# A static attention and convolution schedule: VectorE gets its own dispatcher, PV products lose their order, score groups become two or three, convolution halves are added on VectorE

## Chip, cores, metric

One NeuronCore of a Trainium2 (trn2) chip. The metric is the device time of one execution in microseconds; lower is better. "Fast" and "slow" are states of single runs: a run more than 1.5% above the fastest of the same kernel counts as slow and is left out of ratios. A *ratio* here is the mean time of one kernel's fast runs over the mean of the other's fast runs from the same rounds, so it is not quite the ratio of the medians quoted beside it.

Words used throughout: a *unit* is one block of scores, 128 keys by 512 queries of one head. There are 2048. A *chain* is the five-instruction exponential of one unit on VectorE, which takes it off ScalarE. The *PV product* multiplies a unit's probabilities with the values. A *filler* is a matmul on zeros whose result is not used.

## The reference, cut

```python
# A: short convolution, gate, long convolution (by FFT in the reference), gate
kv = k_shift * v                                   # k_shift: 4-tap causal filter of k; S=2048, D=640
y  = irfft2(rfft2(kv_pad) * rfft2(ssm_k_pad))[:S]  # a causal convolution of length 2048 per channel
a  = q * (y + kv * ssm_D)
# B: attention, 32 heads of 20
q, k, v = split(x @ wqkv)
p = softmax(q @ k.T * 20 ** -0.5)
b = (p @ v) @ wo
return concatenate([a, b], axis=-1)                # bf16 in and out
```

## The kernel before

The program is a list scheduler in Python. It keeps a clock for each engine (`P.T`), asks at each step which piece of work fits, and appends instructions with semaphore waits to each engine's list. What reaches the chip is the fixed order; nothing is decided there. The parts that matter:

```python
# score groups: pairs for the first 48 units, then fixed threes in banks 0-2 and 3-5
while n < NU:
    groups.append((n, min(3, NU - n), n % 6)); n += 3

def EXP_task(t, vec):                       # ScalarE takes 3 units, or 2 and VectorE one
    k, n, b0 = groups[t]; m = n - vec
    P.op("act", exp of m units ...)
    if vec:
        it = vexp_iter(k + m, b0 + m)
        next(it)                            # the chain's first step is put on VectorE's list at once
        chain.append([k + m, it])

def want_vec(t, now):                       # start a chain?
    if n < 3 or len(chain) > 1 or not 140 < k < NU - 30 or P.T["dve"] > now + 0.5:
        return 0
    ...

def PV_task(b):                             # strictly in order of b
    chain_end(4 * b + 3)                    # put the rest of any chain it needs on VectorE's list now
    ...

# end of each of 40 convolution tiles
P.op("dve", tensor_copy(zh, z1)); P.op("dve", tensor_tensor(zl, z1, zh, subtract))   # split into two bf16
for w, n, o, a in ((Win, 64, 0, zh), (Win, 64, 0, zl), (Wc, 60, 4, zh), (Wc, 60, 4, zl)):
    matmul(...)                             # shift by 32 partitions and add in PSUM
P.op("dve", tensor_copy(Y tile, sum))

# in the main loop, when nothing else fits: keep TensorE streaming
if sum(x[1] for x in P.stream) < 2.1 and slack > 0.45 and bnow > 1:
    zeros(...)
```

The kernel divides PSUM into eight banks: 0 to 5 for scores, one for the PV sums and one spare. Projections, transposes, output tiles and the convolution all use the spare one in turn. (cut: loads, first-stage convolution products, tail.)

The softmax here doesn't subtract the row's maximum and nothing guards it: scores larger than these inputs give would overflow.

Of the kernel before, what the change touches and what calls it, by code (L numbers as in the profile page):

```python
# [12 lines left out]
D = 640  # L13
H = 32
DH = 20
# [9 lines left out]
NHK = 5  # L25
# [4 lines left out]
KVPACE, CONV0, CONVE = 3, 500, 80  # L30
# [16 lines left out]
class Buf:  # L47
    def __init__(self, *alias):
        self.w = []
        self.r = []  # L50
        for a in alias:
            self.w += a.w + a.r


def RB(b):

    o = Buf()
    o.w = list(b.r)
    return o


class Prog:
    ENGS = ("sp", "act", "pe", "dve", "pool")

    def __init__(self, nc, enter):
        self.ops = {e: [] for e in self.ENGS}
        self.clock = {e: {} for e in self.ENGS}
        self.cnt = {}
        self.pend = {e: ([], []) for e in self.ENGS}
        self.enter = enter  # L70
        self.plast = None
        self.nc = nc
        self.T = {e: 0.0 for e in self.ENGS}
        self.dma_t = 0.0
        self.gap = None
        self.kind = None
        self.stream = []
        self.sem = {e: self.newsem("s_" + e) for e in self.ENGS if e != "sp"}
# [26 lines left out]
    def ready(self, eng, reads=(), writes=()):  # L105

        own = "s_pe" if eng == "pe" else None
        return max([t[4] for b in reads for t in b.w if t[0] != own] +
                   [t[4] for b in writes for t in b.w + b.r if t[0] != own] + [0.0])

    def op(self, eng, fn, reads=(), writes=(), tok=True, dsem=None, extra=(), n=1, c=0.1, kb=0.0, st=0.0, kind=None):
        own = self.sem[eng][0] if eng in self.sem else None
        if eng == "dve" and self.gap:

            f, self.gap = self.gap, None
            st = self.ready(eng, reads, writes)
            while self.T["dve"] + 0.5 < st and f(self.T["dve"]):
                pass
            self.gap = f
# [17 lines left out]
        if eng == "pe":  # L137
            if kind and kind == self.kind:
                c -= 0.1
            self.kind = kind  # L140
        waits = self._waits(eng, toks)
        start = max([self.T[eng]] + [t[4] for t in toks])
        self.T[eng] = start + c
        if st:
            self.stream.append((start, st))
        when = self.T[eng] + LAT.get(eng, 0.1)
# [63 lines left out]
def build_kernel(nc, A_q, A_k, A_v, A_shift_k, A_ssm_k, A_ssm_D, B_x, B_wqkv, B_wo, out):  # L210
# [3 lines left out]
    with ExitStack() as es:  # L214
# [20 lines left out]
        XI_sb = sb("XI", [128, 2, 512], I32)  # L235
        XZ_sb = sb("XZ", [128, 2, 512], FP32)
        Bout = sb("Bout", [128, 2, D])
# [3 lines left out]
        Win = sb("Win", [128, 128])  # L241
        Wc = sb("Wc", [128, 128])
        ZH = sb("ZH", [128, 2, 256])
        rden = sb("rden", [128, 2, 16], FP32)
# [38 lines left out]
        b_ident, b_Win, b_Wc, b_ones, b_tA, b_tB, b_C = (Buf() for _ in range(7))  # L283
# [5 lines left out]
        b_XI, b_XZ = [Buf(), Buf()], [Buf(), Buf()]  # L289
# [3 lines left out]
        b_On, b_rden = Buf(), [Buf(), Buf()]  # L293
# [29 lines left out]
        P.op("act", lambda e: e.activation(rden[:, 0, :], Zt[:, 0:16], ACT.Exp), reads=[b_Zt], writes=[b_rden[0]], c=1.6)  # L323
# [21 lines left out]
        def b_W(g, which="K"):  # L345
            return (b_WK0 if which == "K" else b_WQ0) if g == 0 else b_Wa if g == 1 else b_Wb


        def mbank():
            return min(mbanks(), key=lambda i: P.ready("pe", (), [bkb[i]]))  # L350

        def mbanks():
            return [MISC] + [OBANK] * (pv[0] == 0) + [4, 5] * (sofar() < NPAIR - 4)

        pv = [0]

        ev_i = [0]

        def XT_part(t, bk, c0, c1, eng, cost):
# [7 lines left out]
            P.op("pe", pe, reads=[b_x(t), b_ident], writes=[bkb[bk]], c=0.05 + 0.06 * (c1 - c0))  # L367
# [4 lines left out]
        def copy(eng, dst, src, bs, bd, cost):  # L372
            if eng == "act":
                P.op("act", lambda e: e.activation(dst, src, ACT.Copy), reads=[bs], writes=[bd], c=cost)
            else:
                P.op("dve", lambda e: e.tensor_copy(dst, src), reads=[bs], writes=[bd], c=cost)  # L376

        def XT_task(t):
            XT_part(t, mbank(), 0, NCC, "dve", 0.5)

        def KQ_mm(which, g, bk, x0, n):
            off = g * 4 * DH
            Wt = WQ if which == "Q" else WKV

            def pe(e):
                for cc in range(NCC):
                    for i in range(4):
                        ins = e.matmul(bank[bk][32 * i:32 * i + DH, 0:n],  # L388
                                       Wt[:, cc, off + i * DH:off + (i + 1) * DH], xT[:, cc, x0:x0 + n],
                                       start=(cc == 0), stop=(cc == NCC - 1), tile_position=(0, 32 * i))  # L390
                return ins
            P.op("pe", pe, reads=b_xT[x0 // 128:(x0 + n + 127) // 128] + [b_W(g, which)], writes=[bkb[bk]],
                 c=0.18 + 1.06 * n / 512, st=1.06 * n / 512)
# [33 lines left out]
        def KQ_task(which, g, c):  # L427
            bk = mbank()
            KQ_mm(which, g, bk, c * 512, 512)
            dst, bd = (QT[:, qs(c, g), :], b_QT[qs(c, g)]) if which == "Q" else (  # L430
                KT[:, g, c * 512:(c + 1) * 512], b_KT[(g, c)])
            copy("dve", dst, bank[bk], bkb[bk], bd, 0.7)
# [3 lines left out]
        def V_task(kb, z):  # L436
            bk = mbank()
            h0, nh = VZ[z]
            w = nh * DH

            def pe(e):
                for cc in range(NCC):
                    ins = e.matmul(bank[bk][:, 0:w], xT[:, cc, kb * 128:(kb + 1) * 128],  # L443
                                   WKV[:, cc, D + h0 * DH:D + h0 * DH + w],
                                   start=(cc == 0), stop=(cc == NCC - 1))
                return ins
            P.op("pe", pe, reads=[b_xT[kb], b_Wa if z == 0 else b_Wb], writes=[bkb[bk]], c=0.05 + 5 * w / 2400,
                 st=5 * w / 2400)
            P.op("dve", lambda e: e.tensor_copy(V_sb[:, kb, h0:h0 + nh, 0:DH],  # L449
                                                bank[bk][:, 0:w].rearrange("p (h d) -> p h d", d=DH)),  # L450
                 reads=[bkb[bk], b_ones], writes=[b_V[(kb, z)]], c=0.17 + w / 960)


        d_kst = [DS("kst0"), DS("kst1")]
        d_kvst = [DS("kvst0"), DS("kvst1")]
        d_kvr, d_sk, d_kext, d_small = DS("kvr"), DS("sk"), DS("kext"), DS("small")
# [11 lines left out]
        def kv_iter():  # L468

            def mul(o, a, b, op, reads, writes):  # L470
                P.op("dve", lambda e: e.tensor_tensor(o, a, b, op), reads=reads, writes=writes, c=0.49)  # L471

            for j in range(KS):
# [3 lines left out]
                     c=0.49)  # L477
# [21 lines left out]
        def setup_pool():  # L499
            P.op("pool", lambda e: e.memset(V_sb[:, :, :, DH:DH + 1], 1.0), writes=[b_ones])  # L500
            for t in (Win, Wc):
                bb = b_Win if t is Win else b_Wc
                P.op("pool", lambda e, t=t: e.memset(t, 0.0), writes=[bb])
                base = 32 if t is Win else -96
                P.op("pool", lambda e, t=t, base=base: e.affine_select(
                    out=t, in_=t, compare_op=ALU.not_equal, fill=1.0, base=base,
                    pattern=[[-1, 128]], channel_multiplier=1), reads=[bb], writes=[bb])
# [18 lines left out]
        groups, n = [], 0  # L526
        while n < NPAIR:
            groups.append((n, 2, n % 4))
            n += 2
        while n < NU:  # L530
            groups.append((n, min(3, NU - n), n % 6))
            n += 3

        def units(t):
            return range(groups[t][0], groups[t][0] + groups[t][1])

        def ubank(t, n):
            return groups[t][2] + n - groups[t][0]

        def S_needs(t):  # L540
            keys = []
            for n in units(t):
                qc, g, kb = qgk(n // 4)
                keys += [("Q", g, qc), ("K", g, kb // 4)]
            return keys

        def S_bufs(t):
            rd, wr = [], []
            for n in units(t):
                qc, g, kb = qgk(n // 4)  # L550
                rd += [x for x in (b_KT[(g, kb // 4)], b_QT[qs(qc, g)]) if x not in rd]
                wr.append(bkb[ubank(t, n)])
            return rd, wr

        def S_task(t):
            def pe(e):
                for n in units(t):
                    (qc, g, kb), u = qgk(n // 4), n % 4
                    ins = e.matmul(bank[ubank(t, n)], KT[32 * u:32 * u + DH, g, kb * 128:(kb + 1) * 128],  # L559
# [3 lines left out]
            rd, wr = S_bufs(t)  # L563
            P.op("pe", pe, reads=rd, writes=wr, c=0.32, st=0.22)

        def EXP_task(t, vec):
            k, n, b0 = groups[t]
            m = n - vec
            P.op("act", lambda e: e.activation(  # L569
                P_sb[:, k % NPU:k % NPU + m, :],  # L570
                PS[:, b0 * 512:(b0 + m) * 512].rearrange("p (u q) -> p u q", u=m), ACT.Exp, scale=scale),
                reads=[bkb[b0 + i] for i in range(m)], writes=[b_P[i % NPU] for i in units(t)[:m]], c=0.066 + 0.4217 * m)
            if vec:
                it = vexp_iter(k + m, b0 + m)
                next(it)
                chain.append([k + m, it])

        chain = []
        vn = [0]

        def vexp_iter(n, bk):


            i = vn[0] % 2
            vn[0] += 1
            XI, XZ, bi, bz = XI_sb[:, i, :], XZ_sb[:, i, :], b_XI[i], b_XZ[i]
# [6 lines left out]
            def step(fn, reads, writes):  # L593
                P.op("dve", fn, reads=reads, writes=writes, c=0.7)

            step(lambda e: e.tensor_scalar(XI, bank[bk], scale * 1.4426950408889634 * w, 127.0 * w, op0=ALU.mult, op1=ALU.add),  # L596
                 [bkb[bk]], [bi])
            yield
            step(lambda e: e.scalar_tensor_tensor(XZ, u, w * c2 / c3, u, op0=ALU.add, op1=ALU.mult), [bi], [bz])  # L599
            yield  # L600
            step(lambda e: e.scalar_tensor_tensor(XZ, XZ, w * w * c1 / c3, u, op0=ALU.add, op1=ALU.mult),  # L601
                 [bi, bz], [bz])
            yield
# [633 lines left out]
```

## Time and profile before

| | |
|---|---|
| time | median 945.38 us of 3 runs (936.87 to 946.68); later 942.39 of 4 |
| profiled run | span 937.6 us, mean granted TensorE clock 0.945 |
| ScalarE floor | 866.4 us (566 exponentials of three units, 125 of two; worked out in the prediction) |
| loss (span less floor) | 71.2 us |
| chains | 100 |
| fillers | 80, none between about 100 us and the end of the convolution |

How to read it: the floor is what ScalarE would take if it never waited. The rest of the span is loss. The prediction shows the lines this rests on; the granted clock by slices (tenths, 40 slices) is the one line that it didn't show:

```profile
PEclk9999999999998999979979999986799999999989
```

The clock records of this trace hold two values, 1.00 and 0.50. A slice is 23.4 us long and a 9 stands for 90% or more of full clock, so a 9 can hide up to 2 x 0.1 x 23.4 = 4.7 us at half clock. The 7s and the 6 are slices where more of the time ran at 0.50.

### The profile page before, as it was taken

What the parts mean: (1) busy time and instruction counts of PE and PEld (TensorE: products, weight loads), DVE (VectorE), ACT (ScalarE), POOL (GpSimd) and SP (SyncE); (2) the same over time, 40 slices, a digit from 0 to 9 for tenths busy, and PEclk for the clock granted to TensorE, in tenths of its full rate; (3) what the DMA queues carried; (4) which work ended last, traced back from release to release, by engine and by line L of the source; (5) the groups of instructions that cost most, each with busy time, mean ns of one, the idle gap of its engine ahead of it and who ended that gap; (6) DMA issues with size and microseconds to landing.
All of it is one profiled execution on the core that took longest, in us unless ns stands there. A gap on an engine that the chain in (4) does not pass through costs nothing.

```text
span 937.6 us, 25931 instructions
## 1 busy us (share of the span) xinstructions
PE 831.5 (89%) x11462; PEld 398.0 (42%) x11464; DVE 597.2 (64%) x1116; ACT 888.0 (95%) x699; POOL 123.9 (13%) x97
## 2 busy tenths in 40 slices
PE   9988888788988999899989999989998898899877
PEld 5333332224544555445535445444454454455222
DVE  4366766646665676866746767775677768667532
ACT  6999999999998999989999999997899999999995
POOL 3000000014220222102202102210202202200000
PEclk9999999999998999979979999986799999999989
DMA  9423343468633675645854656553465556364311
GB/s 288 153 86 122 126 133 119 153 86 206 180 101 108 156 180 155 169 114 140 164 116 126 162 149 167 157 158 94 128 159 150 134 151 154 101 157 122 85 49 52
DMA packets 82012, 129.14 MB, mean 138 GB/s; under 512 B 32977, under 2 KB 58699, under 8 KB 81899
## 3 DMA queue, kind: packets, MB, share of 16 engines
q1 hardware_dynamic: 79739, 124.36, 49.8%
q0 software_dynamic: 704, 2.74, 1.0%
q8 instruction: 90, 1.47, 0.7%
q10 hardware_dynamic: 1456, 0.37, 0.2%
q14 instruction: 23, 0.19, 0.1%
HBM read 116.81 MB, written 13.23 MB: 139 GB/s over the span
## 4 chain that ended last, share of the span: by engine, by line
ACT 62%; PE 30%; DVE 7%; issue 1%; DVEq 0%
ACT P_sb L569 62%; PE PS L859 10%; PE PS L559 8%; PE PS L627 6%; PE PS L388 2%; DVE P_sb L606 1%; PE PS L313 1%; PE PS L701 1%; DVE XZ L601 1%; DVE XI L604 1%; DVE XZ L599 1%; DVE ZH L872 1%; DVE ZH L873 1%; PE PS L880 1%; DVE R L902 0%
## 5 line engine op out<-in xcount | busy, mean ns | idle before, releaser
L569 ACT ACTIVATE P_sb<-PS 128x1536 bf16<-128x1536 f32 (+1 forms) x691 | 883.5, 1461 | 35.3 <-PE PS L559 34.0
L559 PE MATMUL PS<-QT,KT 20*128 20x512 bf16 x2048 | 278.4, 399 | 58.5 <-ACT P_sb L569 53.6
L859 PE MATMUL PS<-R 128*128 128x128 bf16 (+15 forms) x5120 | 244.7, 197 | 2.0 <-DVE O_norm L659 1.1
L859 PEld LDWEIGHTS PS<-R 128*128 128x128 bf16 x5120 | 202.0, 99 | 100.7 <-issue 100.7
L627 PE MATMUL PS<-P_sb,V_sb 128*21 128x512 bf16 x2048 | 174.2, 407 | 17.5 <-DVE P_sb L606 17.1
L827 POOL COPY R<-R 32x512 bf16<-32x512 bf16 x80 | 111.7, 1396 | 500.6 <-PE PS L859 488.7
L559 PEld LDWEIGHTS PS<-QT,KT 20*128 20x128 bf16 x2048 | 67.3, 91 | 212.2 <-ACT P_sb L569 157.8
L596 DVE TENSOR_SCALAR XI<-PS 128x512 int32<-128x512 f32 x100 | 69.1, 691 | 97.7 <-PE PS L559 97.6
L601 DVE SCALAR_TENSOR_TENSOR XZ<-XZ,XI 128x512 f32<-128x512 f32 x100 | 74.0, 740 | 2.4
L606 DVE SCALAR_TENSOR_TENSOR P_sb<-XZ,XI 128x512 uint16<-128x512 f32 x100 | 72.2, 722 | 1.7
L599 DVE SCALAR_TENSOR_TENSOR XZ<-XI 128x512 f32<-128x512 uint16 x100 | 72.2, 722 | 1.0
L627 PEld LDWEIGHTS PS<-P_sb,V_sb 128*21 128x21 bf16 x2048 | 33.2, 90 | 87.5 <-issue 54.7
L471 DVE TENSOR_TENSOR R<-R 128x640 bf16<-128x640 bf16 x128 | 61.4, 486 | 1.9
L604 DVE TENSOR_SCALAR XI<-XI 128x512 int16<-128x512 int16 x100 | 51.3, 513 | 2.0
L376 DVE CAST QT<-PS 128x512 bf16<-128x512 f32 (+1 forms) x32 | 21.8, 681 | 40.9 <-PE PS L388 40.9
L636 DVE CAST OT_sb<-PS 128x512 bf16<-128x512 f32 x32 | 22.1, 690 | 33.8 <-PE PS L627 33.8
L388 PE MATMUL PS<-xT,WQ 128*20 128x512 bf16 (+1 forms) x660 | 42.2, 387 | 0.5 <-DVE QT L376 0.4
L388 PE MATMUL PS<-xT,R 128*20 128x512 bf16 (+2 forms) x660 | 41.4, 381 | 0.5 <-DVE O_norm L659 0.3
L376 DVE CAST KT<-PS 128x512 bf16<-128x512 f32 (+1 forms) x32 | 21.7, 679 | 28.9 <-PE PS L388 28.9
L443 PE MATMUL PS<-R,xT 128*128 128x160 bf16 (+1 forms) x240 | 29.7, 257 | 4.2 <-DVE KT L376 1.4
L449 DVE CAST V_sb<-PS 128x160 bf16<-128x160 f32 (+1 forms) x48 | 18.4, 382 | 21.8 <-PE PS L443 21.4
L872 DVE CAST ZH<-PS 128x256 bf16<-128x256 f32 x40 | 17.0, 425 | 23.1 <-PE PS L859 22.7
(56 smaller groups left out, 351.7 us busy)
## 6 DMA issues: line engine op xcount, KB each, us to landing
R<-kext_scratch SPq DMA_DIRECT2D x640, 132.0 KB, 3.2
R<-in_A_k_dram SPq DMA_DIRECT2D x15, 640.0 KB, 3.9
kext_scratch<-in_A_ssm_k_dram POOLq DMA_DIRECT2D x1, 2560.0 KB, 13.0
R<-in_A_v_dram SPq DMA_DIRECT2D x16, 160.0 KB, 5.4
kv_scratch<-R SPq DMA_DIRECT2D x16, 160.0 KB
kvr_scratch<-R SPq DMA_DIRECT2D x16, 160.0 KB
R<-kvr_scratch SPq DMA_DIRECT2D x8, 320.0 KB, 6.6
R<-in_A_q_dram SPq DMA_DIRECT2D x32, 80.0 KB, 2.0
```

Of the source, the lines that this page charges most:

```text
L388: ins = e.matmul(bank[bk][32 * i:32 * i + DH, 0:n], Wt[:, cc, off + i * DH:off + (i + 1) * DH], xT[:, cc, x0:x0 + n], start=(cc == 0), sto ...
L471: P.op("dve", lambda e: e.tensor_tensor(o, a, b, op), reads=reads, writes=writes, c=0.49)
L559: ins = e.matmul(bank[ubank(t, n)], KT[32 * u:32 * u + DH, g, kb * 128:(kb + 1) * 128], QT[32 * u:32 * u + DH, qs(qc, g), :], start=True, ...
L569: P.op("act", lambda e: e.activation(P_sb[:, k % NPU:k % NPU + m, :], PS[:, b0 * 512:(b0 + m) * 512].rearrange("p (u q) -> p u q", u=m), A ...
L596: step(lambda e: e.tensor_scalar(XI, bank[bk], scale * 1.4426950408889634 * w, 127.0 * w, op0=ALU.mult, op1=ALU.add), [bkb[bk]], [bi])
L599: step(lambda e: e.scalar_tensor_tensor(XZ, u, w * c2 / c3, u, op0=ALU.add, op1=ALU.mult), [bi], [bz])
L601: step(lambda e: e.scalar_tensor_tensor(XZ, XZ, w * w * c1 / c3, u, op0=ALU.add, op1=ALU.mult), [bi, bz], [bz])
L604: step(lambda e: e.tensor_scalar(hi, hi, 128.0, None, op0=ALU.mult), [bi], [bi])
L606: step(lambda e: e.scalar_tensor_tensor(P_sb[:, n % NPU, :].bitcast(U16), XZ, 128.0 * c3 / w ** 3, hi, op0=ALU.mult, op1=ALU.add), [bi, bz ...
L627: ins = e.matmul(bank[OBANK][32 * u:32 * u + DH + 1, :], V_sb[:, kb, 4 * g + u, :], P_sb[:, (4 * b + u) % NPU, :], start=(kb == 0), stop=( ...
L827: P.op("pool", lambda e, dst=dst, src=src: e.tensor_copy(dst, src), reads=[cv["KVr"]], writes=[cv["KVX"][i]] if X == 3 else [], extra=(cv[ ...
L859: P.op("pe", lambda e, o=o, lhsT=lhsT, rhs=rhs, st=st, last=last: e.matmul(o, lhsT, rhs, start=st, stop=last, skip_group_check=True), read ...
```

## The change

Its intent: let VectorE take more units from ScalarE, and let nothing else stand in the way. (1) VectorE no longer gets instructions in the order in which they were thought of; a queue of pending work is served by readiness and priority. (2) PV products of a group run in any order of key blocks, and slots for probabilities come from a free list. (3) A score group is two or three units, and its third bank may be lent to projections. (4) The shift of the convolution's second half is done by two VectorE copies and an addition, not by shift matmuls. (5) Smaller: normalisations of two head groups are merged, output transposes and products repacked, and the filler rule is changed (threshold 1.8 us of streaming in 3.4 us, not 2.1 in 3.2; a convolution matmul counts with its columns alone, not 0.8 of its planned cost; which of the two brings in the fillers is not separated by any run). Projections and output products are also issued in small steps where the old program issued each as one block. Cut to the core:

```diff
-        groups, n = [], 0 ... fixed pairs and threes
+        S_task(ns, b0); EXP_task(k, m, vec, b0, got)      # m = 2 or 3, decided when issued
+    def spare(now):                                       # banks for side work
+            side = [2, 5] if nu[0] < NU - 24 and nu[0] >= NPAIR else []
+            return side + [MISC] * (not conv_wants(now))
-            it = vexp_iter(k + m, b0 + m); next(it); chain.append(...)
+            chain_start(k + m, b0 + m, got[m])            # five steps go to the queue
+    def dve_cands(now):                                   # dispatcher: ready time and priority of each
+        for w in works: ... yield max(T, r), pr, w
+    def want_vec(k, now):
+            if not 60 < k < NU - 34 or len(chains) >= NXB or not xfree: return 0
+            if ((k + 2) // 4) % NKB > 13 or micro_late(now - 1.5): return 0
+            return int(max(0.0, P.T["dve"] - now) + backlog() < VQ)     # VQ = 3.0, NXB = 3
-                    start=(kb == 0), stop=(kb == NKB - 1)
+                    start=first, stop=last                # PV: first and last issued, not by number
-                P.op("pe", four shift matmuls) ; copy
+            work(0.8, [copy M[0:64, 256:512] to ZS[64:128], shifted copy of M[64:128] to ZS[0:64],
+                       Y tile = M + ZS], after)
-                                st=0.8 * cost)
+                            st=2 * n / 2400)
-            if sum(x[1] for x in P.stream) < 2.1 and ...  # over 3.2 us
+            if sum(x[1] for x in P.stream) < ZTH and ...  # ZTH = 1.8, over 3.4 us
```

## The prediction

> **What bounds the kernel now.** I read the page's first two parts, then the chain of work that ended last, then the costliest groups, then the waits, then windows of ten microseconds and short timelines. Shares first:

> ```profile
> PE 831.5 (89%) x11462; PEld 398.0 (42%) x11464; DVE 597.2 (64%) x1116; ACT 888.0 (95%) x699; POOL 123.9 (13%) x97
> ...
> DVE  4366766646665676866746767775677768667532
> ACT  6999999999998999989999999997899999999995
> ...
> ACT 62%; PE 30%; DVE 7%; issue 1%; DVEq 0%
> ```

> ScalarE (ACT) is busy 95% of the span and carries 62% of the chain. VectorE (DVE) is busy 64%, and reaches 80% in only 2 of the 40 slices. ScalarE does nearly one thing, the exponential of 2048 score units of 128x512, except for 100 units that VectorE computes by a five-instruction chain:

> ```profile
> L569 ACT ACTIVATE P_sb<-PS 128x1536 bf16<-128x1536 f32 (+1 forms) x691 | 883.5, 1461 | 35.3 <-PE PS L559 34.0
> ...
> L596 DVE TENSOR_SCALAR XI<-PS 128x512 int32<-128x512 f32 x100 | 69.1, 691 | 97.7 <-PE PS L559 97.6
> L601 DVE SCALAR_TENSOR_TENSOR XZ<-XZ,XI 128x512 f32<-128x512 f32 x100 | 74.0, 740 | 2.4
> L606 DVE SCALAR_TENSOR_TENSOR P_sb<-XZ,XI 128x512 uint16<-128x512 f32 x100 | 72.2, 722 | 1.7
> L599 DVE SCALAR_TENSOR_TENSOR XZ<-XI 128x512 f32<-128x512 uint16 x100 | 72.2, 722 | 1.0
> ...
> L604 DVE TENSOR_SCALAR XI<-XI 128x512 int16<-128x512 int16 x100 | 51.3, 513 | 2.0
> ```

> The exponentials are 566 of three units and 125 of two. From their start times in the trace, the next one starts 1.331 us after one of three and 0.904 us after one of two when nothing is waited for, so a unit costs 0.427 us and an instruction 0.050 us more. The floor is 566 x 1.331 + 125 x 0.904 = 866 us. Summed over all exponentials, the excess over these intervals is 54 us; the other 17 us lie before the first and after the last. 866 + 54 + 17 = 937, the span. VectorE stands idle 97.7 us just before starting a chain: its static order puts the chain's first instruction ahead of other work that could run.

> Where the 54 us are lost is seen by comparing windows (after the time: busy of PE, PEld, DVE, ACT, POOL; granted clock; DMA share; GB/s):

> ```profile
> 400.00:410.00 10.00, 10.00 (x108) 4.98 (x106) 4.79 (x9) 7.05 (x6) 0.10 (x1) 0.50 0.29 71
> ...
> 430.00:440.00 10.00, 8.99 (x153) 4.98 (x150) 5.39 (x10) 10.00 (x10) 2.78 (x3) 1.00 0.16 49
> ```

> At full clock ScalarE is busy all ten microseconds; at half clock TensorE is busy throughout and ScalarE gets only 7.05. The 100 us from 600 lose most (89.21 us of ScalarE work at a mean clock of 0.83). A smaller loss is the PV product waiting for the chain's last step:

> ```profile
> PEld PS L627 <- DVE P_sb L606: 26.2, 33, 3.0
> ...
> PE PS L627 <- DVE P_sb L606: 17.1, 22, 2.7
> ```

> PV products are taken in strict order, [...] so one late chain holds up later scores as well.

> [...] 0.945 over the span means about 2 x 0.055 x 937.6 = 103 us at half rate. [...] of two independent steps the second starts 0.61 us after the first, which lasts 0.69:

> ```profile
> 332.63 0.69 DVE L596 TENSOR_SCALAR XI<-PS 128x512 int32<-128x512 f32 x1 [0.48 <-PE PS L559]
> 333.24 0.68 DVE L601 SCALAR_TENSOR_TENSOR XZ<-XZ,XI 128x512 f32<-128x512 f32 x1
> ```

> [...] the chain's last step has a median of 0.692 us and a maximum of 1.243. [...]

> **The change, part by part.**
> Convolution halves. Now each of 40 tiles makes two VectorE instructions (0.425 + 0.424), four shift matmuls and a third (0.424). After: copy, shifted copy and addition, three of about the same size, so VectorE stays at 40 x 1.27 = 51 us. TensorE loses the shift matmuls, 160 of them at 256 or 240 columns; busy 15.9 + 15.0 = 31 us in the profile, some 17 us of array time, and one round trip per tile through VectorE. TensorE isn't the bound at full clock, so this is slack for scores, worth perhaps 3 us.
> Merged normalisation, transposes and output projection. VectorE's instructions for these fall from 32+32, 16 and 24 to 17+17, 11 and 15; [...] (0.255 us for only 16 elements) it saves about 7 us of VectorE.
> Dispatcher. VectorE's 97.7 us of idle before chains become usable, a chain is begun when VectorE has under 3 us of work queued, three chains may be open in place of two, and chains are allowed from unit 60, not 140. How many chains this gives is the size on which all rests; the schedule decides it, so I estimate it. Chains are possible from about 35 us to 20 us before the end, some 850 us. VectorE's other work is 597.2 - 338.8 (the five rows above) = 258 us, less about 19 outside that stretch and 7 saved: 232. I take VectorE as 91% filled (no chain begins for the last two of every 16 key blocks, when the other VectorE work is late, or when the third bank is lent out): 774 - 232 = 542 us. A chain costs 3.39 us of busy time now; interleaved, it can save up to 5 x 0.08 us and one slow collision, so 2.95. 542 / 2.95 = 184 chains, 84 more than now.
> Groups of two or three. Lending the third bank to projections and taking pairs costs ScalarE more instructions. With 184 threes with a chain, 24 opening pairs, and the remaining 2000 - 552 = 1448 units at a mean of 2.75 (527), there are 735 exponentials, 44 more.
> PV in any order. It takes the 43 us of TensorE and weight-load waiting for chains mostly away. Little of it sets the end: I count it as offset by tighter coupling.
> Sum for ScalarE: (2048 - 184) x 0.427 + 735 x 0.050 = 796 + 37 = 833 us, against 866 before: 33 less. Losses stay at 54 + 17 = 71: time at half clock is not addressed, while less conv work but more scores per microsecond press on TensorE. 833 + 71 = 904. The profile lies at the low end of the three times (936.87 to 946.68, median 945.38), which I lay to the clock; the new kernel should spread likewise, so I add 2: **906 us**, 4% faster.

> **The rivals.**
> (1) VectorE becomes the bound. At 91% it has no reserve for the GpSimd copies (111.7 us in all, and they delay its steps); then scores wait for the bank that a chain hasn't read and PV for chains. For it: the waits above exist already at 64%. Against it: PV may go round a late chain, and chains are only begun on a short queue. It would add 20 to 30 us of losses: 925 to 935.
> (2) TensorE becomes the bound. It is busy 89%, and scores come 4% denser with more small groups and switches. Against it: at full clock windows keep ScalarE at 10.00 of 10, convolution work fills gaps wherever it fits, and the shift matmuls go. If half-clock time grows by half, losses grow by some 15 us: 920.
> (3) The chains don't come. If the lent bank, 24 slots for probabilities or the quota for other work hold them at 130, ScalarE's gain is 30 x 0.427 less the added instructions, about 11 us: 930, within 2%.
> (4) Better: 205 chains (VectorE 96% filled, 2.85 us each) and losses of 55: 787 + 37 + 55 = 879.

> **Range and chances.** (4) gives the low end near 882. (2) and a mild form of (1) give the high end, 926. 2% faster is 926.5, so faster takes nearly all above the lower tail: 0.86 faster, 0.11 within 2%, 0.03 slower.

> **What would show each step.** Chain steps x160 to x210 each; VectorE busy over 85%, its idle before the chain's first step under 40 us; ScalarE busy near 850 us with 700 to 780 exponentials; its waits for scores still 30 to 50 us, mostly at half clock; no shift matmuls; PV waits on chains under 20 us. I am wrong if chains stay under 140, if ScalarE's loss grows past 90 us, or if the chain of work that ended last has VectorE above 25%.

Four statements of the prediction with what the trace of the kernel before shows for them:

- A late chain holds up later scores: in the longest wait of a PV product for a chain, TensorE stood idle for 2.69 us, until 817.03 us, and the next scores started after the PV product, at 817.36.
- Chain steps that ran beside a GpSimd copy took longer (the prediction's delays and slow collision): the last step took a median of 0.857 us in the 17 cases in which it overlapped a copy (L827), and 0.691 in the other 83, at most 0.694. The other three steps that read SBUF alone had medians of 1.18, 1.47 and 0.92 us in the 10, 9 and 12 cases with a copy beside them, against 0.68, 0.69 and 0.46. The first step, which reads PSUM, took 0.692 us with or without one.
- The shift matmuls' array time: back to back at full clock they start 109 to 120 ns apart with 256 columns and 103 with 240 (L880), so 80 x 0.114 + 80 x 0.103 = 17 us.
- The 7 us saved by merging were an estimate; the 0.255 us for 16 elements is the reciprocal (L656).

## The result and the profile after

894.99 us, median of 4 runs (891.19 to 898.71), against 942.39 (936.87 to 946.68, 4 runs): ratio of fast runs 0.949, 95% interval 0.943 to 0.955. On another chip the same kernel ran 888.84 us (6 runs) against 938.78, ratio 0.948. The predicted 906 was 11 us too high, within the range.

The page's first parts, then the chain that ended last:

```profile
PE 835.4 (94%) x11432; PEld 388.0 (44%) x11432; DVE 785.4 (88%) x1427; ACT 856.0 (96%) x737; POOL 126.5 (14%) x94
...
DVE  4569999999699999998999999899999999999752
ACT  6699999999799999998999999999999999999996
...
PEclk9999999999699999999999999999999999999999
...
ACT 48%; DVE 30%; PE 20%; issue 1%; DVEq 0%
```

ScalarE is busy 32 us less (856.0 against 888.0), VectorE 188 us more, and the clock row has one slice that is not a 9. VectorE carries 30% of the last chain against 7% before: it has become a second bound. The costliest groups (busy, mean ns of one, then idle before them):

```profile
L639 ACT ACTIVATE P_sb<-PS 128x1536 bf16<-128x1536 f32 (+1 forms) x729 | 851.5, 1417 | 19.1 <-PE PS L597 18.4
...
L666 DVE TENSOR_SCALAR XI<-PS 128x512 int32<-128x512 f32 x171 | 117.0, 684 | 17.4 <-PE PS L597 16.8
L671 DVE SCALAR_TENSOR_TENSOR XZ<-XZ,XI 128x512 f32<-128x512 f32 x171 | 128.1, 749 | 0.0
L673 DVE SCALAR_TENSOR_TENSOR P_sb<-XZ,XI 128x512 uint16<-128x512 f32 x171 | 120.9, 707 | 4.9
L668 DVE SCALAR_TENSOR_TENSOR XZ<-XI 128x512 f32<-128x512 uint16 x171 | 123.0, 719 | 0.4
L670 DVE TENSOR_SCALAR XI<-XI 128x512 int16<-128x512 int16 x171 | 93.2, 545 | 0.0
...
L348 PE MATMUL PS<-Zt 128*128 128x512 bf16 x208 | 63.6, 402 | 1.5 <-DVE Zt L342 1.0
```

There are 171 chains and 729 exponentials. VectorE's idle time before a chain's first step is 17.4 us, against 97.7. The last line is the one to notice: 208 fillers, where the kernel before had 80. The waits of PV products for a chain's last step (us in total, times, longest):

```profile
PEld PS L692 <- DVE P_sb L673: 16.6, 39, 1.0
...
PE PS L692 <- DVE P_sb L673: 4.8, 14, 0.7
```

21.4 us, against 43.3. A piece of VectorE's timeline (start us, us) shows the dispatcher at work:

```profile
299.87 0.68 DVE L666 TENSOR_SCALAR XI<-PS 128x512 int32<-128x512 f32 x1
300.47 0.45 DVE L670 TENSOR_SCALAR XI<-XI 128x512 int16<-128x512 int16 x1
300.81 0.68 DVE L671 SCALAR_TENSOR_TENSOR XZ<-XZ,XI 128x512 f32<-128x512 f32 x1
301.41 0.68 DVE L702 CAST OT_sb<-PS 128x512 bf16<-128x512 f32 x1
302.01 0.68 DVE L673 SCALAR_TENSOR_TENSOR P_sb<-XZ,XI 128x512 uint16<-128x512 f32 x1
```

Steps of different chains and an evacuation follow each other: after one of 0.68 us the next starts 0.60 us later, after the one of 0.45 us 0.34 us later, so independent neighbours overlap. Over the whole trace the overlap of VectorE instructions is 78 us, against 29 before, so 237 us more of instruction time cost only 188 us more of busy time.

Two terms add up to the change of the profiled span, 48.3 us. By form the exponentials are 419 of three and 310 of two, so the floor is 419 x 1.331 + 310 x 0.904 = 837.9 us, which is 28.5 less. The loss is 889.3 - 837.9 = 51.4 us, which is 19.8 less. The time at half clock, from the clock records of the two traces, fell from 102 to 24 us within the span (the recorded expectations below count whole records, which reach 2 us past its end, and say 104). I had foreseen the first term and not the second, so the experiments ask what each is due to.

### The profile page after: what moved, and what is told of

Its sections match the earlier page's. It is cut to its first block, busy times and chain, and to the rows that moved or that the text cites. A ratio compares the mean times of both kernels' runs of the same rounds, so it can differ in the third digit from the quotient of the medians.

```text
span 889.3 us, 26279 instructions
## 1 busy us (share of the span) xinstructions
PE 835.4 (94%) x11432; PEld 388.0 (44%) x11432; DVE 785.4 (88%) x1427; ACT 856.0 (96%) x737; POOL 126.5 (14%) x94
## 3 DMA queue, kind: packets, MB, share of 16 engines
q8 instruction: 90, 1.47, 0.7%
## 4 chain that ended last, share of the span: by engine, by line
ACT 48%; DVE 30%; PE 20%; issue 1%; DVEq 0%
ACT P_sb L639 48%; PE PS L931 7%; PE PS L597 6%; DVE P_sb L673 5%; DVE XI L666 5%; DVE XZ L668 5%; DVE XZ L671 5%; DVE XI L670 4%; PE PS L692 3%; PE PS L445 2%; DVE R L952 1%; PE PS L348 1%; DVE ZS L950 1%; DVE ZS L949 1%; DVE OT_sb L702 1%
## 5 line engine op out<-in xcount | busy, mean ns | idle before, releaser
L639 ACT ACTIVATE P_sb<-PS 128x1536 bf16<-128x1536 f32 (+1 forms) x729 | 851.5, 1417 | 19.1 <-PE PS L597 18.4
L597 PE MATMUL PS<-QT,KT 20*128 20x512 bf16 x2048 | 286.5, 388 | 30.6 <-ACT P_sb L639 21.7
L666 DVE TENSOR_SCALAR XI<-PS 128x512 int32<-128x512 f32 x171 | 117.0, 684 | 17.4 <-PE PS L597 16.8
L671 DVE SCALAR_TENSOR_TENSOR XZ<-XZ,XI 128x512 f32<-128x512 f32 x171 | 128.1, 749 | 0.0
L673 DVE SCALAR_TENSOR_TENSOR P_sb<-XZ,XI 128x512 uint16<-128x512 f32 x171 | 120.9, 707 | 4.9
L668 DVE SCALAR_TENSOR_TENSOR XZ<-XI 128x512 f32<-128x512 uint16 x171 | 123.0, 719 | 0.4
L670 DVE TENSOR_SCALAR XI<-XI 128x512 int16<-128x512 int16 x171 | 93.2, 545 | 0.0
L692 PEld LDWEIGHTS PS<-P_sb,V_sb 128*21 128x21 bf16 x2048 | 37.6, 89 | 79.4 <-issue 50.4
L348 PE MATMUL PS<-Zt 128*128 128x512 bf16 x208 | 63.6, 402 | 1.5 <-DVE Zt L342 1.0
L530 DVE TENSOR_TENSOR R<-R 128x640 bf16<-128x640 bf16 x128 | 61.6, 487 | 3.7 <-DMA R<-in_A_v_dram 0.9
L445 PE MATMUL PS<-xT,WQ 128*20 128x512 bf16 (+1 forms) x660 | 48.9, 385 | 3.6 <-DVE R L952 1.7
L431 DVE CAST KT<-PS 128x512 bf16<-128x512 f32 (+1 forms) x32 | 21.4, 673 | 11.1 <-PE PS L445 11.1
```

The source lines that it names most:

```text
L348: P.op("pe", lambda e: e.matmul(bank[bk], Zt, zrhs, start=start, stop=start, skip_group_check=True), reads=[b_Zt], writes=[bkb[bk]], tok=s ...
L445: ins = e.matmul(bank[bk][32 * i:32 * i + DH, 0:n], Wt[:, cc, off + i * DH:off + (i + 1) * DH], xT[:, cc, x0:x0 + n], start=(cc == 0), sto ...
L597: ins = e.matmul(bank[b0 + i], KT[32 * u:32 * u + DH, g, kb * 128:(kb + 1) * 128], QT[32 * u:32 * u + DH, qs(qc, g), :], start=True, stop= ...
L639: P.op("act", lambda e: e.activation(P_sb[:, s0:s0 + m, :], PS[:, b0 * 512:(b0 + m) * 512].rearrange("p (u q) -> p u q", u=m), ACT.Exp, sc ...
L666: (lambda e: e.tensor_scalar(XI, bank[bk], scale * 1.4426950408889634 * w, 127.0 * w, op0=ALU.mult, op1=ALU.add), [bkb[bk]], [bl, bh], 0.6 ...
L668: (lambda e: e.scalar_tensor_tensor(XZ, u, w * c2 / c3, u, op0=ALU.add, op1=ALU.mult), [bl], [bz], 0.69, True),
```

## The experiments

Twelve runs were made: the changed kernel again, and eleven edits. "Clock" is the mean granted clock of the fast runs; medians are over all runs. 1, 2, 3, 7, 11 and 12 were run five rounds, the others three. 1 to 4 ran on one chip, 5 to 8 on a second and 9 to 12 on a third, each with the kernel before beside them, so across these groups compare ratios. The scheduler plans anew for each edit: an edit also moves other work, so no run changes one part with all else exactly in place.

| kernel | median us | ratio to before | clock, fast runs | chains | fillers |
|---|---|---|---|---|---|
| before (938.78 to 940.53 in these calls) | | 1 | 0.928 to 0.958 | 100 | 80 |
| after, repeated | 888.84 | 0.948 | 0.977 to 0.994 | 171 | 208 |
| after, no fillers while convolving | 953.88 | 1.014 | 0.887 to 0.896 | 172 | 80 |
| after, more fillers | 891.06 | 0.950 | 0.981 to 0.998 | 171 | 312 |
| after, chains held to 97 | 914.95 | 0.974 | 0.994 to 0.996 | 97 | 322 |
| after, PV in order | 906.28 | 0.963 | 0.977 to 0.989 | 176 | 250 |
| after, no lending (wrong result) | 962.03 | 1.022 | 0.989 to 0.994 | 184 | 384 |
| before, new convolution end | 984.30 | 1.045 | 0.881 to 0.895 | 102 | 112 |
| before, looser chain rule | 971.42 | 1.026 | 0.918 to 0.920 | 103 | 50 |
| before, new convolution end and zeros in its place | 975.63 | 1.037 | 0.912 to 0.922 | 99 | 118 + 80 |
| before, zeros behind the shift matmuls | 952.01 | 1.014 | 0.936 to 0.947 | 104 | 50 + 80 |
| after, PV first at the start | 906.49 | 0.961 | 0.971 to 0.986 | 174 | 214 |
| after, PV first and other settings | 874.43 | 0.933 | 0.994 to 1.000 | 181 | 248 |

**1. The changed kernel again**, no edit, as the yardstick for the next three.

> The changed kernel unaltered, as the yardstick for the three others on the same chip. Expected 890 to 899 us, 171 chains, clock 0.975 to 0.99. If its clock here falls to 0.95 as in the kernel before, the clock difference between the two first profiles was chance and the time should rise to about 905 us.

888.84 us, 1 us below the forecast, at a clock of 0.977 to 0.994. The better clock is not chance: no fast run of the kernel before was above 0.958.

**2. No fillers while convolution tiles remain.**

```diff
-            if sum(x[1] for x in P.stream) < ZTH and slack > 0.45 and bnow > 1:
+            if sum(x[1] for x in P.stream) < ZTH and slack > 0.45 and bnow > 1 and conv_b == 40:
```

> The changed kernel with the filler matmuls on zeros forbidden while convolution tiles remain: 80 zero matmuls instead of 208, as many as the kernel before has, none of them between 100 and 800 us. Chains stay at 172. Theory F (fillers keep the clock up): the granted clock falls to about 0.95, ScalarE loses 10 to 20 us more, time 905 to 915. Theory D (denser real work with fewer switches keeps it up): clock stays at 0.975 or more, time within 4 us of the changed kernel. Theory C (chance): no relation between the fillers and the clock in the repeated runs.

953.88 us: 65 us slower than the changed kernel, and 1.4% slower than the kernel before (interval 0.7 to 2.2%). The profile of a fast run:

```profile
PE 869.5 (91%) x11304; PEld 406.6 (43%) x11304; DVE 792.4 (83%) x1432; ACT 865.5 (91%) x735; POOL 126.0 (13%) x94
...
PEclk9998898899799999999999898897689958657999
...
L639 ACT ACTIVATE P_sb<-PS 128x1536 bf16<-128x1536 f32 (+1 forms) x727 | 861.0, 1339 | 70.3 <-PE PS L597 68.9
```

The floor is unchanged (422 x 1.331 + 305 x 0.904 = 837.4 us), but ScalarE stands idle 70.3 us before its exponentials instead of 19.1 (68.9 and 18.4 of it for scores), and the clock row is dented from end to end: 212 us at half clock. Theory F holds, and by four times the size I had given it. The other theory, that denser work alone keeps the clock up, falls: this kernel has the denser work and the worst clock but one. From the first profile of the changed kernel to this one the loss grows by 113.0 - 51.4 = 61.6 us and half-clock time by 188 us, so each microsecond at half clock costs about a third of one. The traces allow a check: book each exponential's delay beyond 1.331 or 0.904 us to the clock of that moment. At half clock the delays sum to 64.1 us here and 7.4 in the changed kernel, at full clock to 34.0 and 28.3. So all but 6 us of the added delay lies at half clock, and little is left for the new order by itself.

**3. More fillers.**

```diff
-... ZTH ... = 1.8
+... ZTH ... = 2.2          (and the guard described in 5)
```

> The changed kernel with the filler threshold raised from 1.8 to 2.2 us of streaming in the last 3.4 us: 312 zero matmuls instead of 208, 171 chains as before. (It also has a guard that a projection still under way does not count as done; alone, that guard leaves the schedule's counts unchanged.) Theory F: half-clock time goes to nearly nothing (clock 0.99 or more), time 2 to 6 us shorter. Theory D: clock and time unchanged within 3 us, or slightly slower since the fillers take TensorE time.

891.06 us, 2 us from the changed kernel and inside both spreads. The clock rises to 0.981 to 0.998 and nothing is gained: the other part of theory F's forecast, 2 to 6 us, isn't there. 208 fillers already leave little to win.

**4. Chains held to 97.**

```diff
+            if nvec[0] >= 100 * (k - 60) / (NU - 94):
+                return 0
             return int(max(0.0, P.T["dve"] - now) + backlog() < VQ)
```

> The changed kernel with the number of VectorE chains held to 97, spread evenly, everything else kept; the plan then has 531 exponentials of three and 179 of two, so ScalarE's floor is 531 x 1.331 + 179 x 0.904 = 868.6 us against 837.9. If the chains are what shortens ScalarE's work: time rises by about 31 us, to 920 to 930. If the gain came from better packing and not from the chains: less than 10 us slower. If the clock stays high here with few chains, the clock gain is independent of them, and the kernel should still be some 15 us faster than the kernel before.

914.95 us, 26 us above the changed kernel on the same chip, for a floor that is 30.7 us higher. This measures the chains, with one thing beside them: this kernel has 322 fillers, which by 3 moves the time little. It also gives the rest: with 97 chains, about as many as the kernel before, this one is 24 us faster than it. Booked as in 2, its delays at half clock are 2.8 us against 32.6 in the kernel before, and at full clock 25.0 against 22.9, so this rest lies in the clock. Its clock row and last chain:

```profile
PEclk9999999999999999999999999999999999999999
...
ACT 85%; PE 8%; DVE 3%; DMA 1%; POOL 1%; SPq 0%; issue 0%; DVEq 0%
```

With fillers in place and VectorE not pressed, ScalarE carries 85% of the chain, and the loss is 912.1 - 868.6 = 43.5 us, 5 us under that of 1 (48.3), which is why 30.7 us of floor cost only 26. This is what a schedule bound by ScalarE alone looks like.

**5. PV products in order again.**

```diff
-                if V not yet projected: continue
+                if V not yet projected: break
-                if P.ready("pe", rd, ...) <= now + 0.02:
-                    ok.append(b)
+                if P.ready("pe", rd, ...) > now + 0.02:
+                    break
+                ok.append(b)
```

> The changed kernel with PV products forced into the order of the key blocks again, the rest kept: 176 chains, 428 exponentials of three and 294 of two, floor 835 us. If free order matters: TensorE waits for the chain's last step rise from 21 us towards the 43 us of the kernel before, and the time by 5 to 12 us. If it does not: within 3 us of the changed kernel.

906.28 us, ratio 0.963 against 0.948: about 14 us slower, a little more than I allowed. Waits of PV products for the chain's last step rise to 33.6 us (21.4 in the changed kernel). The clock explains little: its run at 0.987 took 903.8 us, and the changed kernel's at 0.988, on the other chip, took 889.0.

A first build of the next experiment read keys before they were written, and was stopped. The scheduler counts a projection as done when its first matmul is placed, so a score may be placed ahead of the projection's end. The shipped order happens not to do that. The guard (a projection under way is not done) leaves the changed kernel's counts of exponentials, chains and fillers unchanged; it is in 3, 6, 11 and 12. 11 and 12 have one guard more: the last PV product of a head group waits for pending normalisations.

**6. No lending of the third bank.**

```diff
-            side = [2, 5] if nu[0] < NU - 24 and nu[0] >= NPAIR else []
+            side = []
```

> The changed kernel without lending: projections, transposes and output tiles get only the one spare bank, while that is not wanted by the convolution. 184 chains, floor 831 us, lower than in the changed kernel. (It has the guard for unfinished projections, without which this order read keys before they were written.) If lending is only a convenience: within 10 us of the changed kernel, since the floor is 7 us lower. If the bank is what lets side work run beside the convolution: the convolution is pushed back, VectorE and TensorE work is left over at the end, 40 to 70 us slower.

The result was wrong (relative error 1.0), so its time counts only as the time of this stream of instructions. A likely cause is that normalisations come so late here that the tile they read is overwritten; I didn't show it, and a guarded version found no schedule (that attempt is not on record). The time, 962.03 us, is 73 us above the changed kernel's on the other chip (ratios 1.022 and 0.948) though the floor is 7 us lower and the clock is 0.99:

```profile
L639 ACT ACTIVATE P_sb<-PS 128x1536 bf16<-128x1536 f32 (+1 forms) x695 | 844.1, 1465 | 99.3 <-PE PS L597 98.8
```

ScalarE's waits for scores are 98.8 us. In the longest, 9.6 us up to 693.45 us, TensorE finishes a convolution tile in the spare bank, then computes a query projection in that bank, and only then the scores that need it. As far as a kernel with a wrong result can tell, nothing of the gain would be left without the lending.

**7. The new convolution end alone, in the kernel before** (with the layout of the first-stage products that it needs).

```diff
-                copy, subtract, four shift matmuls, copy
+                copy M[0:64,256:512] -> ZS[64:128]; shifted copy M[64:128] -> ZS[0:64]; Y = M + ZS
```

> The kernel before with only the convolution's end changed: two copies into a float tile and an addition on VectorE in place of two copies, four shift matmuls and a copy. 102 chains, floor 865.5 us against 866.4. My step: TensorE was not the bound, so 0 to 5 us faster, 934 to 942. Rival: the shift matmuls and their round trip held the spare bank long enough to cost more, 8 to 15 us faster.

984.30 us, 4.5% slower than the kernel before, where I had said 0 to 5 us faster. The floor is about the same (865.5), the fast runs' clock is 0.881 to 0.895. The clock row of the profiled run, which was a slow one (995.3 us; its time is not used):

```profile
PEclk9999999997879886867689999698786977877988
```

**8. A looser rule for chains, in the kernel before.**

```diff
-  len(chain) > 1 or not 140 < k < NU - 30 or P.T["dve"] > now + 0.5
+  len(chain) > 1 or not 60 < k < NU - 30 or P.T["dve"] > now + 1.5
```

> The kernel before with only its rule for starting chains loosened: from unit 60 instead of 140 and with VectorE up to 1.5 us behind instead of 0.5. If VectorE's idle time alone was the resource, this should give more chains and a faster kernel. The old fixed groups with the old order give only 103 chains, and I expect the chains to sit in front of evacuations that TensorE needs: 15 to 30 us slower than the kernel before, which would show that the dispatcher, not the rule, makes the chains possible.

971.42 us over its four runs, 964 in the two fast ones, with 103 chains. As expected: at this setting the old fixed order places hardly more chains though it is allowed to. Its clock fell too (0.92), so the slowdown is not only the chains' place.

**9 and 10. Was it the shift matmuls that kept the clock up?** In 9, two zero matmuls of 512 columns stand where the four shift matmuls stood; in 10 they are added to the kernel before. Back to back at full clock, matmuls on zeros of 512 columns start 216 ns apart in the trace before (L313), so 80 of them are some 17 us.

```diff
+  for _ in range(2):
+      matmul(bank[MISC], Zt, zrhs, start=False, ...)      # adds zero
```

> The kernel with only the convolution's end moved to VectorE (984 us, 266 us at half clock), and at the place of the four shift matmuls of each tile two matmuls on zeros of 512 columns, that add zero to the convolution's bank: 80 in all, some 17 us of array time and no result. Theory A (the shift matmuls were dense work that kept the clock up, and their loss is what made that kernel slow): half-clock time falls from 266 us to about 100 to 150, time 940 to 955. Theory B (the new convolution end is itself slower in the old order, through its VectorE waits): half-clock time and time stay, 975 or more.

> The kernel before, with two matmuls on zeros of 512 columns added behind the four shift matmuls of each of the 40 tiles. Theory A: half-clock time falls from 104 us to 30 to 60. ScalarE's loss beyond its floor of 865 us should follow the relation seen so far, about 45 us plus 0.32 us for each us at half clock, so 55 to 65 us: 922 to 935 us. Against it: the old order has TensorE full at full clock, and the 17 us more array time push the convolution later (the plan grows by 13 us), so the time may stay at 940 although the clock is better.

The first took 968 to 977 us in its three fast runs, clock 0.912 to 0.922, so about 163 us at half clock (2 x 0.084 x 973) against about 221 (2 x 0.1126 x 982) in the fast runs of 7. That is the direction of theory A at half its size at most, and only 9 us. The second was slower than the kernel before, 952.01, at a clock no better. So dense work put in at one fixed place is not the cure, and theory A explains a part at most. Why the order with the new end has so many thin windows stays open.

One run of 9, the profiled one, had a span of 1626.5 us and is listed with a clock of 1.000. But its trace holds no clock record at all, and the 1.000 only says that none was found. Its matmuls tell more (line, shapes, count, then busy us, mean ns of one):

```profile
L551 PE MATMUL PS<-QT,KT 20*128 20x512 bf16 x2048 | 454.6, 668 | 2.2 <-ACT P_sb L561 2.0
L619 PE MATMUL PS<-P_sb,V_sb 128*21 128x512 bf16 x2048 | 318.2, 697 | 13.9 <-DVE P_sb L598 13.7
```

668 and 697 ns where the kernel before has 399 and 407, and consecutive full-array matmuls of 512 columns never start less than 0.36 us apart, where 0.216 is usual at full clock (L313 in the trace before; 0.427 at half clock). This run is in no comparison, though the median in the table counts it.

**11. PV ahead of side work when slots run short, at the start.** The changed kernel has one exponential that waits 7.0 us near 23 us. Its timeline there shows 24 units' probabilities waiting (all slots full) while TensorE does projections for 8 us before the first PV product.

```diff
+            ok, nrem = pv_ready(now)
+            if ok and bnow < 14 and len(free) < 8:
+                PV_task(ok[0]); continue
```

> The changed kernel with one more rule: in the first 14 key blocks, when fewer than 8 slots for probabilities are free, a PV product goes ahead of projections (and guards so that unfinished projections and pending normalisations hold their readers and overwriters back). 174 chains, floor 836.8 us, 214 zero matmuls. ScalarE's one wait of 7.0 us near 23 us should go, and the span fall by 3 to 6 us, to 882 to 886 (890 at the most if later waits take it back).

906.49 us, ratio 0.961: slower, where I expected 3 to 6 us faster. The only profile is of a slow run (914.5 us), so it shows where time can go and not why the fast runs are slower too; and the guard for normalisations came in with the rule. Windows of this kernel, then of the changed one (columns as in the prediction):

```profile
0.00:50.00 50.00, 47.62 (x615) 23.12 (x616) 22.16 (x51) 41.93 (x44) 7.86 (x12) 1.00 0.72 224
...
200.00:300.00 100.00, 93.49 (x1017) 41.53 (x1016) 77.92 (x123) 81.38 (x71) 20.73 (x14) 0.74 0.47 111
```

```profile
0.00:50.00 50.00, 47.72 (x606) 24.09 (x606) 22.60 (x55) 34.84 (x38) 7.87 (x12) 1.00 0.72 223
...
200.00:300.00 100.00, 95.25 (x1297) 45.02 (x1298) 88.91 (x147) 93.82 (x82) 26.85 (x18) 0.90 0.63 154
```

The repair did what it should: ScalarE gets 41.93 us of work into the first 50, against 34.84. Then this run goes to half clock at 200 to 300 us (0.74) and loses 12 us of ScalarE's work there. In the fast runs the clock is 0.971 to 0.986 and the time 897 to 908; what makes them slower than the changed kernel stays open.

**12. The same with other settings**, picked from 132 combinations by the scheduler's own plan, among those with 200 to 250 fillers (the search is not on record; six of the settings change at once, and no run separates them).

```diff
-KV0, KVPACE, APACE, VQ, CONVE, ZTH, AGE, WAIT3 = 30.0, 0.75, 0.5, 3.0, 80, 1.8, 9, 0.3
+KV0, KVPACE, APACE, VQ, CONVE, ZTH, AGE, WAIT3 = 35.0, 0.7, 0.5, 2.5, 60, 2.0, 26, 0.3
```

> The same rule and guards, with the schedule's settings moved: a late chain is hurried after 26 units instead of 9, the filler threshold 2.0 instead of 1.8, the chain queue 2.5 us instead of 3.0, the convolution spread to the last 60 units instead of 80, the shift products a little later. 181 chains, floor 832.6 us, 248 zero matmuls, TensorE's plan 9 us shorter. Expected 876 to 884 us at a clock of 0.98 or more, that is 5 to 12 us faster than the changed kernel. If VectorE, then filled to 90% or more, runs later than planned, PV waits rise and it is no faster than 886.

874.43 us (873.29 to 878.13, 6 runs), ratio 0.933: correct, and faster than both kernels; by the ratios it is 1.6 to 1.8% below the changed one.

```profile
PE 826.8 (95%) x11460; PEld 386.7 (44%) x11472; DVE 793.4 (91%) x1477; ACT 850.2 (97%) x725; POOL 124.6 (14%) x94
...
PEclk9999999999999999999999999999999999999999
```

No slice is below full clock (1.000 over the span), and ScalarE is busy 97% of the span. 181 chains give a floor of 832.6 us; the loss is 39.8 us, the smallest of all.

| streaming in the window | windows | next window at half clock |
|---|---|---|
| under 38% | 32 | 32 |
| 38% to 45% | 42 | 33 |
| 45% to 50% | 54 | 5 |
| 50% or more | 2375 | 0 |

The kernel before has 15 windows under 45%, the changed kernel 3 (3 when repeated), the one without fillers 19, the best one 1. The longest idle stretch of TensorE in the profile before is 2.7 us, in a trace with 102 us at half clock. This is a relation in the traces together with one direct test of its cause (2). The limits were read off after the fact, and with the grid shifted by 0.3 us either way up to 5 of 40 windows in the first row stay at full clock and up to 2 in the last do not; the exact rule behind them isn't shown.

## Why the prediction was right, and where it was not

**ScalarE's floor (right).** Predicted 184 chains and 735 exponentials, 833 us; there were 171 and 729, 837.9 us. Experiment 4 measures this term: 26 us of time for 30.7 us of floor. It is a little over half of the gain of 50 us on that chip.

**VectorE filled to 91% at 2.95 us a chain (both right; its other work was set too low).** In the window from 35 to 870 us VectorE is busy 763.5 of 835 us, 91%. A chain's five rows cost 582.2 / 171 = 3.40 us, but the prediction credits overlap to the chains. Done so with the measured trace, the other instructions' own time is 281 us and a chain costs (785.4 - 281.3) / 171 = 2.95 us. The slip was in the other work: 597.2 - 338.8 = 258 us had the 29 us of overlap of the kernel before already taken off, while its instructions last 288. The 7 us that I had estimated for merging came (7.1), and the slower addition took 6 of them back. 30 us more of other work is 10 of the 13 chains that are missing.

**"Losses stay at 54 + 17 = 71: time at half clock is not addressed" (wrong; this is the step that failed).** The loss fell to 51.4 us, because half-clock time fell from 102 to 24 us. I had read the new filler rule in the change as a moved threshold and costed nothing for it. The changed kernel has 128 more fillers, and experiment 2 shows what they are worth in the changed kernel: 65 us. At a third of a microsecond each, 79 us less at half clock gives 26 us; about 7 are given back by the new wait at the start (7.0 us), which I hadn't foreseen either. 26 - 7 is 19, and the measured fall is 19.8. Booked as in 2, the two traces say the same: delays at half clock fell from 32.6 to 7.4 us, those at full clock rose from 22.9 to 28.3.

**Convolution halves "worth perhaps 3 us" (wrong when alone).** Alone they cost 44 us (7), by an estimate some 40 of them through the clock: 221 us at half clock against 102 in the first profile, at a third of a microsecond each. VectorE's side of it: 16.7 + 16.4 + 23.9 = 57 us against my 51, because the addition takes 598 ns (586 to 622 in 40 of 40 cases, L952), where the copy whose place it takes took 424 (L886). In the kernel before, a subtraction of one PSUM and one SBUF input without a stride took 424 ns (L873), and the copy reads PSUM with the same stride as the addition, so neither the mixed inputs nor the PSUM stride alone costs more; the strided float input from SBUF is what is left, and no run tests it alone. In the changed kernel this loss can't be seen; that the fillers stand in for the shift matmuls fits 2, but no run tests it by itself.

**PV in any order "counted as offset by tighter coupling" (too low).** Taken back, it costs about 14 us (5).

**Rival 2, TensorE through the clock**, was the right rival with the wrong sign: the clock was the second largest term, but the change improved it. Rival 3 is out (171 chains), and rival 1 is half true: the mark that I had set for it, VectorE above 25% of the last chain, was passed at 30% without the time suffering, so the mark was a poor one. Two more of its signs were missed: ScalarE's waits for scores, predicted at 30 to 50 us, are 18.4, and PV waits on chains, predicted under 20, are 21.4.

**Right in time, partly by luck of signs**: a floor 5 us too low, a loss 20 us too high and 2 us added for spread in place of 6 came out 11 us too high.

## What to carry to other kernels

In a schedule that TensorE does not bound, look at how much it streams in each 3.4 us and not only at how busy it looks: under 38% the next window always ran at half clock here (32 of 32), from 50% on never (0 of 2375), and matmuls on zeros in otherwise empty places were worth more than any other part that was tested with a right result (65 us, experiment 2). A change that takes matmuls out can cost more through the clock than it saves (7: 44 us slower, at a clock of 0.881 to 0.895 against 0.928 to 0.950 beside it), so test it with the clock row in view. And when an engine is to take work off another, give it a queue that is served by readiness: loosening the old rule made 3 more chains, the queue with its free slots and lent bank made 71. No run has the queue without the slots and the bank, or these without it.
